# Which transfer GpSimd shares out at the start: half of dV of pair 0, or half of K of pair 2

## The chip, the cores and the metric

One NeuronCore of a Trainium2 chip. The metric is the device time of one execution in microseconds (us), taken as the median of several runs. PE is TensorE, DVE is VectorE, ACT is ScalarE, POOL is GpSimd and SP is SyncE. Sixteen DMA engines move all data between HBM and the on-chip memory (SBUF); SP's and POOL's transfers run on the same sixteen, from queues of their own. MB and KB are powers of two here where a transfer's size is meant.

## The reference

Attention of one query row per head, forward and backward, in bf16. There are 32 heads, 8192 keys each, and 128 features.

```
q: [1, 32, 1, 128]   k, v: [1, 32, 8192, 128]   grad_out: [1, 32, 1, 128]
scores = einsum('bhqd,bhkd->bhqk', q, k) * 128 ** -0.5
attn   = softmax(scores)
out    = einsum('bhqk,bhkd->bhqd', attn, v)
returns out, and the gradients dq, dk, dv of it for grad_out
```

K and V are read once (134 MB), dK and dV, of the same size, are written once. dV is the outer product of the weights with grad_out's row; dK is the outer product of the scores' gradient with q's row.

## The kernel before, in words

Heads are worked on in 16 pairs (`j`). K and V of a pair are 4 MB each and lie in SBUF as 128 partitions of 128 rows, 32 KB to a partition. Three K tiles and two V tiles rotate. dV overwrites V in place and dK overwrites K in place, in eight steps `r` of 16 rows (`outer`, L286; DVE at L290), and the result is stored from the same tile. So a tile comes free for the next load when its store has landed.

For a pair, DVE transposes K blocks (`k_blocks`, L188) and PE makes scores of them (L198). DVE, ACT and PE make the softmax (L422 to L455). PE turns V (`v_transposes`, L215; ACT copies, L220) and multiplies it with grad_out (L232). Then DVE writes dV. The scores' gradient (`ds_of`, L320) and dK follow in the next turn of the loop (`p_ = j - 1`). For the first pairs (`early`), the first half of V of pair `j` is turned between the gradient of pair `j - 1` and its dK (L401). The order is written out by hand (`tc.manual_schedule`, L126); each engine takes its instructions in that order, and the order of issue on SP is that of the program.

Transfers: K, V, dV and dK go through SP's queue, one 4 MB transfer each, or in parts where `LOADS` (L25) and `ENDS` (L18) say so: K of pair 0 in four, V of pair 0 in two, V of pair 1 in four, K of pair 2 in two; some stores in two or three. A transfer of 128 partitions gives each of the 16 DMA engines 8 partitions. The first five loads (K 0, V 0, K 1, V 1, K 2) are issued at the start (L98 to L102).

The exception is dV of pair 0. Its first half (64 of the 128 rows of each partition, 2 MB, so 16 KB from each partition) is stored by POOL, when four of the eight steps are done (L297, `share_out` at L116). Its six transfers take 39, 42, 8, 25, 10 and 4 partitions (`SHARES`, L27). The program counts on this: POOL's transfer of n partitions is spread over the largest number up to 16 that divides n, here 13, 14, 8, 5, 10 and 4 engines, beginning with the one at which a cursor stands, and moves the cursor on by as many. Between them, `turn_to` (L107) issues copies of a few bytes into `turned` that move the cursor to the engine that SHARES names first. By that count the engines 0 to 15 get

```
engine  0  1  2  3  4  5  6  7  8  9 10 11 12 13 14 15
rows   12 12 12  6  0  4  7  8  8  8  9  8  8  7  7 12      (partitions' 16 KB; 128 in all)
```

The second half of dV of pair 0 is stored by SP after the eighth step (L299). The two small outputs (out_0 and out_1, 8 KB each) are stored by POOL near the end (L404, L406, `result` at L334).

Of the kernel before, what the change touches and what calls it, by code (L numbers as in the profile page):

```python
# [18 lines left out]
CH = 16  # L19
# [2 lines left out]
K_BUFS = 3  # L22
V_BUFS = 2
QD = 32
LOADS = {("k", 0): 4, ("v", 0): 2, ("v", 1): 4, ("k", 2): 2}  # L25
SHARED = 64
SHARES = ((6, 12, 39), (5, 2, 42), (5, 1, 8), (15, 55, 25), (10, 25, 10), (7, 0, 4))  # L27
GP = 4

# [2 lines left out]
def kernel(  # L32
# [11 lines left out]
    nc = tc.nc  # L44
# [5 lines left out]
    NT = 2 * S // P  # L50
    NU = NT // CH
# [21 lines left out]
    Kt, Vt, XK, XV, st, acc, qd = {}, {}, {}, {}, {}, {}, {}  # L73

    def rows_of(x, j, c=0, parts=1):
        L = NT // parts
        return x[0, 2 * j:2 * j + 2].rearrange("b s d -> (b s) d").rearrange("(p n) d -> p n d", p=P)[:, c * L:(c + 1) * L, :]

    def slots(X, c, parts):
        L = NT // parts  # L80
        return X[:, c * L:(c + 1) * L, :]

    def load_k(j):
        parts = LOADS.get(("k", j), 1)
        Kt[j] = kpool.tile([P, NT, D], BF16, tag="K", name="Kt")
        for c in range(parts):
            nc.sync.dma_start(slots(Kt[j], c, parts), rows_of(k, j, c, parts))

    def load_v(j):
        Vt[j] = vpool.tile([P, NT, D], BF16, tag="V", name="Vt")  # L90
        parts = LOADS.get(("v", j), 1)
        for c in range(parts):
            nc.sync.dma_start(slots(Vt[j], c, parts), rows_of(v, j, c, parts))

    rows = consts.tile([H, 2, D], BF16)
    nc.scalar.dma_start(rows[:, 0, :], q.rearrange("b h s d -> (b h s) d"))
    nc.scalar.dma_start(rows[:, 1, :], grad_out.rearrange("b h s d -> (b h s) d"))
    load_k(0)  # L98
    load_v(0)
    load_k(1)  # L100
    load_v(1)
    load_k(2)  # L102

    turned = consts.tile([17, len(SHARES), 2, 2], BF16)
    cursor = [0, 0]

    def turn_to(engine):  # L107
        n = (engine - cursor[0]) % 16
        if n:
            rows = n if n > 1 else 17  # L110
            nc.gpsimd.dma_start(turned[0:rows, cursor[1]],  # L111
                                k[0, 0].rearrange("(p n) d -> p n d", p=P)[0:rows, 0:2, 0:2])
            cursor[1] += 1
        cursor[0] = engine

    def share_out(dst, src):  # L116
        for engine, first, n in SHARES:
            turn_to(engine)
            last = first + 3 * n - 2
            nc.gpsimd.dma_start(dst[first:last:3], src[first:last:3], max_dma_last_dim=8192)  # L120
            cursor[0] = (cursor[0] + max(i for i in range(1, 17) if n % i == 0)) % 16
# [14 lines left out]
    nc.gpsimd.memset(do_win[:], 0.0)  # L136
    win = consts.tile([P, NG, 2 * QD - 8], BF16)
    nc.gpsimd.memset(win[:], 0.0)
    in_quad = consts.tile([P, NQ], F32)
    nc.vector.reduce_sum(in_quad[:], ident[:].rearrange("p (a i) -> p a i", a=NQ), axis=AX.X)  # L140

# [26 lines left out]
    o_all = consts.tile([P, H], F32)  # L168
    dq_all = consts.tile([P, H], F32)
# [99 lines left out]
    def gather_copy(j, which):  # L269
        if j % GP != GP - 1:  # L270
            return
        S = acc["S" + which] = small.tile([P, 4, D], F32, tag="S", name="S_" + which)
        nc.scalar.copy(S[:].rearrange("p j d -> p (j d)"), acc.pop(which)[:])

    def gather(j, which, bank):
        if j % GP != GP - 1:
            return
        S, to = acc.pop("S" + which), (o_all if which == "p" else dq_all)
        pick = lane[:].rearrange("p (w j) -> p j w", j=4)
        at = 8 if which == "p" else 16  # L280
        for i in range(4):
            nc.tensor.matmul(bank[:, at:at + 2 * GP], lhsT=S[:, i, :], rhs=pick[:, i, :],
                             start=(i == 0), stop=(i == 3), skip_group_check=True)
        nc.scalar.copy(to[:, 2 * (j - GP + 1):2 * j + 2], bank[:, at:at + 2 * GP])

    def outer(j, which, r):  # L286
        x = st[j]
        G, dst = (Kt[j], out_2) if which == "dk" else (Vt[j], out_3)
        rep, row = x["ds"] if which == "dk" else x["p"], qd[j][:, 0 if which == "dk" else 1, :]
        nc.vector.tensor_tensor(  # L290
            slots(G, r, NU).rearrange("p n (a b) -> p n a b", b=R),
            slots(rep, r, NU).unsqueeze(2).to_broadcast([P, CH, D // R, R]),
            row.rearrange("p (a b) -> p a b", b=R).unsqueeze(1).to_broadcast([P, CH, D // R, R]),
            op=ALU.mult)
        if (which, j) == ("dv", 0):
            if (r + 1) * CH == SHARED:
                share_out(rows_of(dst, 0)[:, 0:SHARED, :], G[:, 0:SHARED, :])  # L297
            elif r == NU - 1:
                nc.sync.dma_start(rows_of(dst, 0)[:, SHARED:NT, :], G[:, SHARED:NT, :])  # L299
            return  # L300
        ends = ENDS.get((which, j), (8,))
        if r + 1 in ends:
            i = ends.index(r + 1)
            a, b = (ends[i - 1] if i else 0) * CH, (r + 1) * CH
            nc.sync.dma_start(rows_of(dst, j)[:, a:b, :], G[:, a:b, :])
# [25 lines left out]
        nc.vector.tensor_copy(x["ds"][:], ds1[:].unsqueeze(2).to_broadcast([P, NT, R]))  # L331
        window(ds1[:].rearrange("p (g j) -> p g j", j=4))

    def result(src, dst, issuer):  # L334
        half = small.tile([P, H], BF16, tag="half", name="half", bufs=2)
        nc.scalar.copy(half[:], src[:])
        fin_ps = psT.tile([P, 2 * TB, P], BF16, tag="T", name="fin_ps")
        nc.tensor.transpose(fin_ps[0:H, 0, :], half[:], ident[:])
        fin_sb = small.tile([H, D], BF16, tag="fin", name="fin_sb", bufs=2)
        nc.scalar.copy(fin_sb[:], fin_ps[0:H, 0, :])  # L340
        issuer.dma_start(dst.rearrange("b h s d -> (b h s) d"), fin_sb[:])

    DQ = NG // 4
    NC = NX // TB
# [5 lines left out]
    def half(j, f):  # L350
        for c in range(f * NC, (f + 1) * NC):
            chunk(j, c)
        v_scores(j, f)

    for j in range(HP + 1):
# [42 lines left out]
        if ends and j > 0:  # L398
            gather_copy(p_, "ds")
            if early:  # L400
                half(j, 0)  # L401
            for r in range(NU):
                if j == HP and r == NU - 2:
                    result(o_all, out_0, nc.gpsimd)  # L404
                    gather(p_, "ds", st[p_]["m"])
                    result(dq_all, out_1, nc.gpsimd)  # L406
                outer(p_, "dk", r)
            if j + 1 < HP:
                load_v(j + 1)
# [7 lines left out]
        if not ends:  # L417
            gather_copy(p_, "ds")
            outer(p_, "dk", 0)
            outer(p_, "dk", 1)  # L420
# [104 lines left out]
```

## Time and profile before

| what | value |
|---|---|
| median of 3 runs | 633.09 us (632.57 to 633.21) |
| the profiled execution: its own time | 632.87 us |
| its span, first to last instruction | 631.1 us |
| busy: PE, DVE, ACT, POOL | 73%, 82%, 32%, 2% |
| bytes moved by DMA, mean rate | 268.98 MB, 426 GB/s |
| HBM read, written | 134.23 MB, 134.23 MB |
| q1 (SP's queue): packets, MB | 11232, 266.34 |
| q0 (POOL's queue): packets, MB | 800, 2.12 |

The prediction uses the page (its slices of DMA share and GB/s, its queues), the timelines of SP, POOL and DVE, and stretches of a few us. In a timeline a line begins with its start and its length in us, then engine, source line, operation and what it writes from what; in brackets stands the engine's idle time before it and what ended that. SPq lines are issues of transfers, not the transfers themselves. A stretch shows the busy time of PE, weight loads, DVE, ACT and POOL, then TensorE's granted clock, the DMA engines' mean busy share and GB/s. Beside these the trace has a record for each DMA packet (start, length, size, queue), which doesn't name the engine but lets one follow it, since an engine's next packet starts some 3 ns before the last one's end; and 16 landing records for each transfer, one for each engine.

### The profile page before, as it was taken

The page shows a single profiled execution, that of the slowest core. Times are in us where ns is not written, and L with a number is a line of the kernel's source. Part 1 is how long each engine was busy: PE and PEld are TensorE (multiplying, and loading weights), DVE is VectorE, ACT ScalarE, POOL GpSimd, SP SyncE. Part 2 cuts the span into 40 slices and gives each one's busy share as a digit, 9 for nine tenths or more (in the row PEclk, how much of TensorE's full clock was granted, in tenths as well). Part 3 has the DMA queues.
Part 4 walks back from the last instruction along what each step waited for, and adds up shares of the span by engine and source line. Part 5 has one row for each costly group of instructions (what it writes and reads, how often), then busy time and mean ns, then how long its engine had stood idle before and what let it go on. Part 6 is the DMA issues. An engine that isn't in the chain of part 4 may idle for free.

```text
span 631.1 us, 8018 instructions
## 1 busy us (share of the span) xinstructions
PE 462.9 (73%) x3256; PEld 245.9 (39%) x3256; DVE 516.4 (82%) x654; ACT 205.1 (32%) x460; POOL 11.3 (2%) x23
## 2 busy tenths in 40 slices
PE   4887678878787788676888757867679776697671
PEld 1443344244443425233363432624336243262441
DVE  6579997989889798796879959879697895987973
ACT  2432424043342505134052330613316142160431
POOL 2040000000000000000000000000000000000000
PEclk9789987789798977788868789777897778987785
DMA  8999999999999999999999999999999999999997
GB/s 366 433 402 436 430 428 431 429 427 440 433 427 436 436 431 433 433 432 429 429 432 429 427 433 427 433 432 418 431 430 437 436 431 425 436 427 431 428 426 336
DMA packets 12164, 268.98 MB, mean 426 GB/s; under 512 B 1856, under 2 KB 1888, under 8 KB 1888
## 3 DMA queue, kind: packets, MB, share of 16 engines
q1 hardware_dynamic: 11232, 266.34, 98.5%
q0 software_dynamic: 800, 2.12, 0.8%
q8 instruction: 25, 0.41, 0.2%
q14 instruction: 11, 0.09, 0.0%
q10 hardware_dynamic: 96, 0.02, 0.0%
HBM read 134.23 MB, written 134.23 MB: 425 GB/s over the span
## 4 chain that ended last, share of the span: by engine, by line
issue 91%; DMA 3%; PE 3%; DVE 1%; ACT 0%; POOL 0%; POOLq 0%; ACTq 0%
DMA out_dram<-Vt 2%; PE s_ps L198 1%; DMA Kt<-in_k_dram 1%; PE T_ps L215 1%; PE acc_p L265 0%; DVE XK_sb L188 0%; DVE Vt L290 0%; POOL out_dram L120 0%; DVE q_blk L174 0%; ACT p_rep L452 0%; DVE sT L205 0%; ACT win L255 0%; ACT e L440 0%; POOL turned L111 0%; POOLq L520 0%
## 5 line engine op out<-in xcount | busy, mean ns | idle before, releaser
L198 PE MATMUL s_ps<-XK_sb,q_win 128*128 128x512 bf16 x512 | 152.4, 432 | 66.6 <-DVE XK_sb L188 61.3
L290 DVE TENSOR_TENSOR Vt<-p_rep,qd 128x2048 bf16<-128x2048 bf16 x128 | 154.0, 1223 | 40.1 <-PE acc_p L265 32.2
L188 DVE STREAM_TRANSPOSE XK_sb<-Kt 128x1024 f32<-128x1024 f32 x128 | 150.2, 1218 | 37.7 <-DMA Kt<-in_k_dram 35.0
L215 PE MATMUL T_ps<-ident_f,Vt 128*128 128x128 f32 x1024 | 165.4, 314 | 6.1 <-DMA Vt<-in_v_dram 6.1
L220 ACT COPY XV_sb<-T_ps 128x512 f32<-128x512 f32 x256 | 139.6, 591 | 82.6 <-PE T_ps L215 82.4
L290 DVE TENSOR_TENSOR Kt<-ds_rep,qd 128x2048 bf16<-128x2048 bf16 x128 | 149.5, 1215 | 3.2 <-PE acc_ds L265 2.8
L215 PEld LDWEIGHTS T_ps<-ident_f,Vt 128*128 128x128 f32 x1024 | 131.2, 160 | 43.8 <-issue 18.7
L198 PEld LDWEIGHTS <-q_win 128*128 128x128 bf16 x512 | 51.6, 110 | 155.6 <-issue 123.9
L265 PE MATMUL acc_p<-Vt,win 128*32 128x512 bf16 x512 | 55.9, 439 | 2.8 <-ACT win L255 2.8
L440 ACT ACTIVATE e<-sT,nbias 128x128 f32<-128x128 f32 x16 | 8.2, 515 | 150.6 <-DVE nbias L436 150.6
L265 PEld LDWEIGHTS <-win 128*32 128x32 bf16 x1024 | 23.0, 99 | 60.6 <-issue 49.4
L265 PE MATMUL acc_ds<-Kt,win 128*32 128x512 bf16 x512 | 42.7, 429 | 4.6 <-ACT win L255 4.6
L232 PE MATMUL dp_ps<-XV_sb,do_win 128*32 128x512 bf16 x512 | 34.3, 383 | 13.5 <-ACT XV_sb L220 13.5
L255 ACT COPY win<-ds 64x128 bf16<-64x128 bf16 x32 | 9.5, 296 | 106.4 <-DVE ds L327 106.2
L232 PEld LDWEIGHTS <-do_win 128*32 128x32 bf16 x512 | 14.3, 94 | 29.2 <-issue 22.5
L441 PE MATMUL m_ps<-rs,ones_f 128*128 128x1 f32 x32 | 7.5, 305 | 24.4 <-ACT e L440 24.4
L427 PE MATMUL m_ps<-ident_f,top 128*128 128x128 f32 x16 | 4.8, 300 | 23.5 <-DVE top L425 23.5
L205 DVE STREAM_TRANSPOSE sT<-s_ps 128x512 f32<-128x512 f32 x16 | 11.5, 717 | 10.7 <-PE s_ps L198 10.7
L441 PEld LDWEIGHTS m_ps<-rs,ones_f 128*128 128x128 f32 x32 | 6.2, 242 | 27.6 <-ACT e L440 27.6
L452 ACT ACTIVATE p_rep<-e,rinv 128x512 bf16<-128x512 f32 x16 | 11.5, 722 | 13.3 <-DVE rinv L450 13.3
L427 PEld LDWEIGHTS m_ps<-ident_f,top 128*128 128x128 f32 x16 | 2.1, 133 | 31.0 <-issue 25.4
L317 PEld LDWEIGHTS m_ps<-pd,ones_f 128*128 128x128 f32 x32 | 8.2, 276 | 10.6 <-DVE prod L248 9.8
(60 smaller groups left out, 158.1 us busy)
## 6 DMA issues: line engine op xcount, KB each, us to landing
Kt<-in_k_dram SPq DMA_DIRECT2D x14, 4096.0 KB, 29.1
Vt<-in_v_dram SPq DMA_DIRECT2D x14, 4096.0 KB, 29.0
out_dram<-Kt SPq DMA_DIRECT2D x13, 4096.0 KB, 25.1
out_dram<-Vt SPq DMA_DIRECT2D x13, 4096.0 KB, 32.3
out_dram<-Vt SPq DMA_DIRECT2D x5, 2048.0 KB, 16.2
out_dram<-Kt SPq DMA_DIRECT2D x5, 2048.0 KB, 15.7
Kt<-in_k_dram SPq DMA_DIRECT2D x4, 1024.0 KB, 8.2
Vt<-in_v_dram SPq DMA_DIRECT2D x2, 2048.0 KB, 17.5
```

The source lines that it names most:

```text
L188: nc.vector.transpose(XK[j, u][:].rearrange("p g w i -> p (g w i)"), slots(Kt[j], u, NU).rearrange("p g d -> p (g d)").bitcast(F32))
L198: nc.tensor.matmul(st[j]["s"][:], lhsT=q_win[:, c, at:at + P], rhs=cols[:, c // 2, c % 2], start=(u == 0 and c == 0), stop=(u == NU - 1 an ...
L205: nc.vector.transpose(sT[:].rearrange("p g r -> p (g r)"), x["s"][:])
L215: nc.tensor.transpose(T_ps[:, i, :], words[:, m * P:(m + 1) * P], ident_f[:])
L220: nc.scalar.copy(XV[j][:, b * TB:(b + 1) * TB, :], st[j].pop(("T", c))[:])
L232: nc.tensor.matmul(out[b * QD:(b + 1) * QD, :], lhsT=do_win[:, b // 2, e2, at:at + QD], rhs=cols[:, z, e2, :, b * QD:(b + 1) * QD], start= ...
L255: nc.scalar.copy(win[t * M:(t + 1) * M, :, at:at + 4], src[t * M:(t + 1) * M])
L265: nc.tensor.matmul(acc[which][b * QD:(b + 1) * QD, :], lhsT=win[:, g, at:at + QD], rhs=X[:, 4 * g:4 * g + 4, :].rearrange("p n d -> p (n d)"),
L290: nc.vector.tensor_tensor(slots(G, r, NU).rearrange("p n (a b) -> p n a b", b=R), slots(rep, r, NU).unsqueeze(2).to_broadcast([P, CH, D // ...
L317: nc.tensor.matmul(x["m"][:, 1:3], lhsT=ones_f[:], rhs=x["pd"][:], start=True, stop=True, skip_group_check=True)
L441: nc.tensor.matmul(x["m"][:, 0:1], lhsT=ones_f[:], rhs=rs[:], start=True, stop=True, skip_group_check=True)
L452: nc.scalar.activation(x["p"][:], e[:].unsqueeze(2).to_broadcast([P, NT, R]), ACT.Copy, scale=rinv[:])
```

## The change

POOL no longer stores anything. It loads the second half of K of pair 2 (64 rows of each partition, 2 MB) with the same `SHARES`, the same cursor copies and the same partitions, right after its memsets at the start, where it waits for nothing else. SP loads only the first half of that tile, in one transfer. dV of pair 0 is stored whole by SP after the eighth step, like other dV. V of pair 1 is loaded in one transfer, no longer four, and V of pair 0 in four, no longer two. The two small outputs are stored by SP: out_0 and out_1 stand between the second and the third part of the last dK store in SP's order.

SP's order at the start becomes K 0 in four parts, V 0 in four, K 1, V 1, half of K 2, dV 0, dK 0, V 2, and then as before. The instructions of PE, DVE and ACT are the same in number and order.

```diff
-LOADS = {("k", 0): 4, ("v", 0): 2, ("v", 1): 4, ("k", 2): 2}
+LOADS = {("k", 0): 4, ("v", 0): 4}
 SHARED = 64
+SHARED_K = 2
...
     def load_k(j):
         parts = LOADS.get(("k", j), 1)
         Kt[j] = kpool.tile([P, NT, D], BF16, tag="K", name="Kt")
+        if j == SHARED_K:
+            nc.sync.dma_start(Kt[j][:, 0:NT - SHARED, :], rows_of(k, j)[:, 0:NT - SHARED, :])
+            return
...
-    def share_out(dst, src):
+    def share(dst, src):
...
     nc.gpsimd.memset(win[:], 0.0)
+    share(Kt[SHARED_K][:, NT - SHARED:NT, :], rows_of(k, SHARED_K)[:, NT - SHARED:NT, :])
...
-        if (which, j) == ("dv", 0):
-            if (r + 1) * CH == SHARED:
-                share_out(rows_of(dst, 0)[:, 0:SHARED, :], G[:, 0:SHARED, :])
-            elif r == NU - 1:
-                nc.sync.dma_start(rows_of(dst, 0)[:, SHARED:NT, :], G[:, SHARED:NT, :])
-            return
...
-    def result(src, dst, issuer):
+    def result(src, dst):
...
-        issuer.dma_start(dst.rearrange("b h s d -> (b h s) d"), fin_sb[:])
+        nc.sync.dma_start(dst.rearrange("b h s d -> (b h s) d"), fin_sb[:])
...
-                    result(o_all, out_0, nc.gpsimd)
+                    result(o_all, out_0)
...
-                    result(dq_all, out_1, nc.gpsimd)
+                    result(dq_all, out_1)
```

## The prediction, made before the change was run

> **What bounds it now.** I read the page's slices first, then the DMA part, the windows of the two places where the rate falls, and the timelines of SP (SyncE, the queue that issues), POOL and DVE.
>
> ```profile
> span 631.1 us, 8018 instructions
> ...
> DMA  8999999999999999999999999999999999999997
> GB/s 366 433 402 436 430 428 431 429 427 440 433 427 436 436 431 433 433 432 429 429 432 429 427 433 427 433 432 418 431 430 437 436 431 425 436 427 431 428 426 336
> ...
> q1 hardware_dynamic: 11232, 266.34, 98.5%
> q0 software_dynamic: 800, 2.12, 0.8%
> ```
>
> The 16 DMA engines are busy in every slice, at 425 to 440 GB/s in nearly all; DVE, the next, is at 82%. Only three slices are lower: first, third, last. So the time is the bytes (268.98 MB in both kernels), plus what an engine stands idle, plus how unevenly the 16 finish. The chain of waits tells nothing here (91% "issue"). q0 is GpSimd's queue, q1 SyncE's.
>
> ```profile
> 34.00:36.00 2.00, 2.00 (x20) 1.25 (x18) 1.87 (x2) 1.69 (x4) 2.00 (x4) 1.00 1.03 348
> 36.00:38.00 2.00, 1.60 (x20) 1.09 (x20) 1.74 (x3) 1.53 (x3) 0.92 (x2) 1.00 0.98 356
> ...
> 626.00:628.00 2.00, 0.00 (x0) 0.00 (x0) 0.00 (x0) 0.00 (x0) 0.00 (x0) 0.50 0.65 279
> 628.00:630.00 2.00, 0.00 (x0) 0.00 (x0) 0.00 (x0) 0.00 (x0) 0.00 (x0) 0.50 0.19 82
> ```
>
> The last two columns are the DMA engines' busy share and GB/s. At 34 to 38 us, where GpSimd's transfers begin, the engines are busy yet slow: (4 - 2*348/430 - 2*356/430) = 0.7 us lost by all. At the end they finish one by one. The trace's landing records (16 for a transfer, one an engine) of the last store run from 626.7 to 630.2, middle 628.2.
>
> **What the share does.** SyncE's transfers give each engine the same bytes; GpSimd's do not. By SHARES, engines 0, 1, 2 and 15 get 12 rows of 16 KB, most of the others 7 to 9, engine 3 gets 6, engine 5 gets 4 and engine 4 none. The landing records agree: those of one transfer spread over 0.7 us up to 22 us, and over 7.1 us from 57 us on, with one engine about 3 us ahead of the next. I call it the front engine. In the packet records it takes 1246 ns for 32 KB of a store where the others take 1213, so it falls back 8*33 = 0.27 us in each 4 MB store, 8.6 us over 32 stores. Its last landing is 629.4, the twelfth of 16. So the share is a head start that the front engine has used up at the end; moving it from 32 us to 4 us changes neither its rows nor the sum.
>
> **Part by part.**
>
> 1. *Bytes and packet sizes.* Per engine and 4 MB, start to start in the packet records: 32 packets of 8 KB by 0.306 = 9.79 us; 16 of 16 KB by 0.610 = 9.76; 8 of 32 KB by 1.210 = 9.68. V of pair 0 goes from 16 to 8 KB: +0.03. V of pair 1 from 8 to 32 KB: -0.11. K of pair 2 has half of its 16 KB turned to GpSimd's 8 KB: +0.02; dV of pair 0 goes from half 8, half 16 to 32 KB: -0.10. Sum **-0.16 us**.
>
> 2. *The share itself.* The same 12 issues of GpSimd, with the same rows, in the same order, so 0.7 us of slow packets again, now at about 7 to 9 us. The trace has no shared load, only shared stores; bounds are -0.7 (a load doesn't do it) and +0.7 (twice as much). I take **0**: the slow packets were SyncE's own, ahead of the first shared byte at 36.3.
>
> 3. *What the share delays at the start.* GpSimd now has nothing to wait for but its memsets:
>
> ```profile
> 3.44 0.73 POOL L111 DMA_DIRECT2D turned<-in_k_dram  x1
> 32.13 0.65 POOL L120 DMA_DIRECT2D out_dram<-Vt  x1 [27.97 <-DVE Vt L290]
> ...
> 36.35 0.57 POOL L111 DMA_DIRECT2D turned<-in_k_dram  x1
> 41.53 0.56 POOL L120 DMA_DIRECT2D out_dram<-Vt  x1 [4.61 <-DMA out_dram<-Vt]
> ```
>
> Its first share is issued at 3.44+0.73 = 4.2 and, with the 4.2 us from issue (32.13) to first byte (36.3), moves from 8.3 on. In the packet records from 36 us on an engine alternates: one packet of q0, one of q1, 1:1, where q0's small packets (cursor copies, completions) take a turn but only 9 ns. Engine 0 gets six 8 KB packets, 3 small ones, six, about 5 small, ten, and so on. K of pair 0 lands in four parts, at 5.8, 8.4, 10.8 and 13.3 us. At 8.3 the slowest engine has some 6.5 packets of part 3 to go and 8 of part 4. Part 3: 6 of q0 in between, 10.8 + 6*0.306 + 0.7 (point 2) = 13.4. Part 4: 12 of q0 ahead of its last, 13.3 + 12*0.306 + 0.7 = 17.7.
>
> ```profile
> 12.70 2.37 DVE L188 STREAM_TRANSPOSE XK_sb<-Kt 128x1024 f32<-128x1024 f32 x2 [0.15 <-PE s_ps L198]
> 15.82 2.37 DVE L188 STREAM_TRANSPOSE XK_sb<-Kt 128x1024 f32<-128x1024 f32 x2 [0.74 <-PE s_ps L198]
> 19.31 0.72 DVE L205 STREAM_TRANSPOSE sT<-s_ps 128x512 f32<-128x512 f32 x1 [1.12 <-PE s_ps L198]
> ```
>
> Part 3 is used at 12.70 and part 4 at 15.82, so all computing shifts by D = 17.7 - 15.82 = **1.9 us**. Ends: 0.5 (the share comes late) and 5.5 (all 24 packets, 7.3 us, ahead of part 4: 13.3+7.3+0.7-15.82). I take 1.9, as the alternation is in the records. [...]
>
> 4. *Who hides D: the backlog in the rings.* SyncE's issues are early; the question is whether one comes after the front engine has run dry (its landing, the first of 16, less the 0.5 us that the record lags) less 1.0 us from issue to first packet (0.74 to 1.75 at the start).
>
> ```profile
> 38.77 0.35 SPq L299 DMA_DIRECT2D out_dram<-Vt  x1
> 52.89 0.34 SPq L305 DMA_DIRECT2D out_dram<-Kt  x1
> 65.04 0.34 SPq L93 DMA_DIRECT2D Vt<-in_v_dram  x1
> 73.17 4.87 SPq L305 DMA_DIRECT2D out_dram<-Vt  x2
> ```
>
> The front engine has no share, so it is dry at the same bytes in both kernels: after 18 MB at 47.5, 22 MB at 57.8, 30 MB at 77.5 (landings). dV of pair 0, whole: may come at 46.0, comes at 38.8+D. dK of pair 0: 56.3 against 52.9+D. dV of pair 1: 76.0 against 73.2+D. So the cover is 7.2, 3.4 and **2.8 us**, later 5.0 (dK 1), 3.1 (dV 2) and 3.7 (dK 2), and from 147 us on over 8. The other engines have 2.4 us more (4 rows). V of pair 2 (65.0 against 66.3) waits for the landing of dV 0 on the slowest engine; that engine has had the same bytes, so it stays. Were the cover gone, the front engine's end moves by D-2.8, and 0.8 of that is free (629.4 against 630.2). At D = 1.9: **0**.
>
> 5. *V of pair 1 whole.* PE turns its first half at 46.5+D = 48.4; whole, it lands on engine 0 at 1.9 + 64*0.306 + 24*0.306 + 2*9.68 + 0.7 + 0.5 = 49.4. PE waits 1 us, behind it the scores of pair 1; those wait for DVE, busy with dK of pair 0 to 52.8+D, and PE was done 1.7 us before DVE. Hidden: **0**.
>
> 6. *The two small outputs* go from POOL's queue to SP's, ahead of the last dK store. SP then issues that at 620.3+0.4 to +0.8. The first five engines run dry at about 621.4 and idle up to 0.8 us; they landed 3 us before the last: **0**.
>
> **Sum.** -0.16 on the profiled execution: its span is 631.1 and its time 632.87 (1.8 around it), so **632.7 us**. The median of the three runs is 633.09; a difference under 0.2% (1.3 us) is about what can't be told from none.
>
> **Rivals.**
>
> *Starved front engine (slower).* The share gets ahead of part 4. Against: 1:1 alternation. For: the issue comes while q1 has 8 KB packets, and contention at 34 to 38 us is not understood. It decides from D = 2.8+0.8 = 3.6; at D = 5.5 the end is 1.9 us later: 634.6.
>
> *The load sprays otherwise (slower).* The head starts hang on the engine at which a shared transfer begins, and on how many it uses. Before shows this for stores only. If a load with n rows begins at engine 0 with n/16 rows each, rounded up, the front engine gets 3+3+1+2+1 = 10 rows, 10*0.61 = 6.1 us: it ends at 635.5 in place of 630.2, in all 632.87+5.3 = 638.2. Against: the small "turned" copies are loads, and moved the cursor as counted. [...]
>
> *A better share (faster).* The slow packets of 34 to 38 us go (-0.7) and the last engines land nearer the middle (630.2 against 628.2, so at most -1.9): with -0.16 and half of the second, 631.0. For: nothing is stored while the share moves. Against: the rows are the same.
>
> *Worse balance at the end (slower).* The instruction fetches, 16 KB packets that cost their engine 0.9 us each, meet other engines than before; two more on the last engine: 634.5.
>
> **Numbers.** Forecast 0.52, all of it within 0.2%; starved 0.15; other spray 0.10; better share 0.15; worse balance 0.08. Faster 0.15, same 0.52, slower 0.33. The range runs from 631.0 to 636.0: it leaves out the other spray and some of the better share.
>
> **What would show it.** DVE's first transposes of part 4 at about 17.7; landings of the first V of pair 0 spread by several us; the front engine some 7 us ahead by 30 us; dK of pair 0 issued near 54.8 and no slice under 420 GB/s after the second; last landings again over some 3.5 us, ending near 630. An idle front engine between 57 and 78 us, or another order of finishing, would make it wrong.

## The result, and the profile after

The changed kernel takes **643.84 us** (median; 643.33 to 645.03) where the kernel before took 633.14 on the same chip. The ratio is 1.0172, 95% interval 1.0159 to 1.0185: slower by 10.7 us. I had forecast 632.7 us, no change, with a range from 631.0 to 636.0.

The page of the kernel after: its span, the DMA part of the slices, the two large queues.

```profile
span 642.0 us, 8013 instructions
...
DMA  8999999999999999999999999999999999999996
GB/s 296 269 391 433 432 419 435 435 432 429 430 432 434 433 428 434 432 431 430 438 433 428 429 429 432 430 429 436 434 429 426 429 434 436 427 430 432 425 427 293
...
q1 hardware_dynamic: 11040, 266.36, 97.9%
q0 software_dynamic: 736, 2.10, 1.2%
```

The bytes are the same 268.98 MB, and the DMA engines are as busy as before. But in the first three slices they move 296, 269 and 391 GB/s, where before had 366, 433 and 402; from the fourth on all is as it was. q0 takes 1.2% of the engines' span, where nearly the same bytes cost 0.8% before: its packets last longer. Stretches of four us show where this begins and ends (columns as before: the last two are the DMA engines' busy share and GB/s).

```profile
4.00:8.00 4.00, 0.80 (x4) 0.40 (x4) 2.32 (x3) 0.90 (x4) 4.00 (x8) 1.00 1.02 426
8.00:12.00 4.00, 2.77 (x7) 1.00 (x8) 2.81 (x11) 0.26 (x1) 0.90 (x2) 1.00 1.04 295
...
16.00:20.00 4.00, 2.06 (x8) 0.77 (x8) 1.30 (x2) 0.00 (x0) 0.47 (x1) 1.00 1.03 264
...
32.00:36.00 4.00, 2.41 (x15) 1.67 (x14) 2.09 (x2) 1.73 (x5) 0.00 (x0) 0.65 1.02 264
36.00:40.00 4.00, 3.87 (x26) 2.12 (x28) 2.11 (x2) 1.76 (x3) 0.00 (x0) 0.50 1.08 440
```

```profile
8.00:36.00 28.00, 16.96 (x74) 7.79 (x75) 12.45 (x24) 6.69 (x19) 2.62 (x5) 0.89 1.03 275
```

And the same 28 us of the kernel before:

```profile
8.00:36.00 28.00, 23.25 (x141) 12.45 (x141) 17.57 (x28) 11.27 (x28) 3.87 (x7) 0.88 1.01 424
```

The slow stretch begins with the first shared packet (8.1 us in the packet records) and ends with the last (35.5). The second block takes it as one: 275 GB/s, where the kernel before has 424. The loss is 28*(1 - 275/430) = **10.1 us**. It falls on both queues: between 8 and 36 us a packet of 8 KB took 471 ns on average in GpSimd's queue and 488 ns in SyncE's, where before had averages of 311 and 313 at 38 to 60 us.

What the engines compute is late as well. First SP's issues after, then DVE's transposes of the third and fourth part of K of pair 0:

```profile
47.38 0.35 SPq L304 DMA_DIRECT2D out_dram<-Vt  x1
65.34 0.34 SPq L304 DMA_DIRECT2D out_dram<-Kt  x1
...
86.12 4.88 SPq L304 DMA_DIRECT2D out_dram<-Vt  x2
```

```profile
14.93 2.37 DVE L193 STREAM_TRANSPOSE XK_sb<-Kt 128x1024 f32<-128x1024 f32 x2 [2.54 <-DMA Kt<-in_k_dram]
21.39 2.37 DVE L193 STREAM_TRANSPOSE XK_sb<-Kt 128x1024 f32<-128x1024 f32 x2 [4.09 <-DMA Kt<-in_k_dram]
```

Part 4 is used at 21.4 us (before 15.8, forecast 17.7), and dV of pair 0 goes out at 47.4 (before 38.8, forecast 40.7). Most of this comes free, because the DMA engines are late by as much and the rings (the engines' queues) do not run dry: from 40 to 615 us the packet records show fewer than 16 packets under way for only 0.3 us in all. The front engine alone falls back. Its lead over the middle landing shrinks by 1.0 us at 98 us and by 0.4 at 108, and its last packets there are longer: 1007 and 1208 ns for 16 KB, where 611 is usual, and 1533 for 32 KB, where 1213 is. Why these packets are long is not shown. At the end the 16 landings of the last store run from 636.6 to 641.1, middle 637.9. The middle is 9.7 us later than before (628.2), the last landing 10.9 (630.2). So about 10 us are the slow packets, and about 1 us the wider spread at the end.

### The profile page after: what moved, and what is told of

Its sections match the earlier page's. It is cut to its first block, busy times and chain, and to the rows that moved or that the text cites. A ratio compares the mean times of both kernels' runs of the same rounds, so it can differ in the third digit from the quotient of the medians.

```text
span 642.0 us, 8013 instructions
## 1 busy us (share of the span) xinstructions
PE 466.0 (73%) x3256; PEld 248.7 (39%) x3256; DVE 516.2 (80%) x654; ACT 204.9 (32%) x460; POOL 10.0 (2%) x21
## 2 busy tenths in 40 slices
DMA packets 11908, 268.98 MB, mean 419 GB/s; under 512 B 1888, under 2 KB 1888, under 8 KB 1888
## 4 chain that ended last, share of the span: by engine, by line
DMA 57%; PE 23%; DVE 14%; ACT 3%; issue 1%; DVEq 0%; ACTq 0%; SPq 0%
DMA Vt<-in_v_dram 32%; DMA out_dram<-Vt 15%; PE T_ps L220 12%; DMA Kt<-in_k_dram 7%; DVE Kt L295 5%; PE s_ps L203 5%; DVE Vt L295 4%; PE acc_p L270 3%; DVE XK_sb L193 3%; DMA out_dram<-Kt 3%; ACT XV_sb L225 2%; PE dp_ps L237 2%; PE acc_ds L270 1%; DMA rows<-in_grad_out_dram 1%; DVE sT L210 1%
## 5 line engine op out<-in xcount | busy, mean ns | idle before, releaser
L203 PE MATMUL s_ps<-XK_sb,q_win 128*128 128x512 bf16 x512 | 155.0, 440 | 72.0 <-DVE XK_sb L193 67.4
L220 PE MATMUL T_ps<-ident_f,Vt 128*128 128x128 f32 x1024 | 168.4, 318 | 8.1 <-DMA Vt<-in_v_dram 8.1
L220 PEld LDWEIGHTS T_ps<-ident_f,Vt 128*128 128x128 f32 x1024 | 134.8, 163 | 45.7 <-issue 21.4
L270 PE MATMUL acc_p<-Vt,win 128*32 128x512 bf16 x512 | 56.2, 442 | 2.9 <-ACT win L260 2.9
L237 PEld LDWEIGHTS <-do_win 128*32 128x32 bf16 x512 | 14.5, 95 | 29.3 <-issue 22.9
```

What stands on the lines that cost most here:

```text
L203: nc.tensor.matmul(st[j]["s"][:], lhsT=q_win[:, c, at:at + P], rhs=cols[:, c // 2, c % 2], start=(u == 0 and c == 0), stop=(u == NU - 1 an ...
L220: nc.tensor.transpose(T_ps[:, i, :], words[:, m * P:(m + 1) * P], ident_f[:])
L237: nc.tensor.matmul(out[b * QD:(b + 1) * QD, :], lhsT=do_win[:, b // 2, e2, at:at + QD], rhs=cols[:, z, e2, :, b * QD:(b + 1) * QD], start= ...
L270: nc.tensor.matmul(acc[which][b * QD:(b + 1) * QD, :], lhsT=win[:, g, at:at + QD], rhs=X[:, 4 * g:4 * g + 4, :].rearrange("p n d -> p (n d)"),
```

## The experiments

Three theories stood at the start, and two came later; the expectations name them by letters. **A**: a transfer is slow while it writes SBUF partitions into which another DMA engine is loading at the same time. **B**: any GpSimd load beside SyncE's loads slows both. **C**: the cursor copies or the uneven shares do it. **P**, a sharper A: the partitions fall into sets of eight, each of which takes about what one DMA engine brings; time is lost when two engines write into one set at once, whatever their queue. **F**: an engine that writes partitions other than those it gets in a transfer of 128 (call those its own, the others foreign) is slow by itself. Each kernel starts from the one after, and each ratio is to the kernel before, measured on the same chip. In the one after, a shared transfer takes every third partition of a range (`dst[first:last:3]` in `share`), so by the program's count the partitions that fall to an engine are not those of a transfer of 128.

**1. No share.** K of pair 2 is loaded whole by SyncE.

```diff
-        if j == SHARED_K:
-            nc.sync.dma_start(Kt[j][:, 0:NT - SHARED, :], rows_of(k, j)[:, 0:NT - SHARED, :])
-            return
...
-    share(Kt[SHARED_K][:, NT - SHARED:NT, :], rows_of(k, SHARED_K)[:, NT - SHARED:NT, :])
```

> The changed kernel without the share: K of pair 2 whole by SP, POOL moves nothing; every engine gets the same bytes. Three theories for the 10.7 us that the change cost, all in the stretch from 8 to 36 us where the DMA rate fell from 430 to about 270 GB/s. A, foreign partitions: a shared load writes partitions that another engine's load is writing at the same time. B, two load queues: any load of POOL beside SP's loads slows both. C, the cursor copies and uneven transfers of POOL. All three expect 430 GB/s from 8 to 36 us here, and the front engine (slow on stores) to end 8 rows * 0.61 = 4.9 us later than before the change: about 637 us. So a shared load would be worse than no share.

Measured: 636.79 us, ratio 1.0058 (1.0043 to 1.0073).

```profile
8.00:12.00 4.00, 2.87 (x7) 1.00 (x8) 2.81 (x10) 0.26 (x1) 0.00 (x0) 1.00 1.01 426
```

The last landings run from 629.5 over 4.6 us, with one engine last by 1.9 us, as is to be expected of the front engine without its head start. So the share as a load costs 7 us against no share at all, and the share as a store, with the parts that the loads had before, had brought 3.7.

**2. The share as a store again,** with the other edits of the change kept.

```diff
+        if (which, j) == ("dv", 0):
+            if (r + 1) * CH == SHARED:
+                share(rows_of(dst, 0)[:, 0:SHARED, :], G[:, 0:SHARED, :])
+            elif r == NU - 1:
+                nc.sync.dma_start(rows_of(dst, 0)[:, SHARED:NT, :], G[:, SHARED:NT, :])
+            return
```

(and experiment 1's edit)

> The changed kernel with the share put back to the first half of dV of pair 0, as before; the rest of the change stays (V of pair 0 in four parts, V of pair 1 in one, K of pair 2 in one, small outputs by SP). A, B and C: all the loss goes, 632.7 us within 1.3, and 430 GB/s from 8 to 30 us. If the parts of loads or the outputs' queue cost anything, it shows here: 634 or more.

Measured: 644.48 us, ratio 1.018 (1.0165 to 1.0196). A miss, and not for the reason of the changed kernel: from 8 to 30 us the rate is 439 GB/s, as before. SP's issue of V of pair 2, and the stretches beside it:

```profile
76.11 0.34 SPq L94 DMA_DIRECT2D Vt<-in_v_dram  x1
```

```profile
66.00:70.00 4.00, 3.33 (x40) 1.92 (x40) 3.20 (x4) 3.32 (x9) 0.00 (x0) 1.00 0.91 379
70.00:74.00 4.00, 3.61 (x37) 1.82 (x34) 4.00 (x4) 2.04 (x6) 0.00 (x0) 1.00 0.56 174
74.00:78.00 4.00, 2.10 (x10) 0.87 (x8) 3.45 (x8) 0.00 (x0) 0.00 (x0) 1.00 0.48 129
```

Here the busy share falls too (0.56, 0.48): the engines are idle. V of pair 2 is issued at 76.1, before at 65.0, as it waits for dV of pair 0 to leave its tile. In the packet records of before the two queues alternate packet by packet: of GpSimd's 256 packets of 8 KB, 186 have a single packet that starts 2 to 5 ns before their end, and in all 186 cases it is SyncE's, 104 of 8 KB, 57 of 16 KB and 25 of 4 bytes. V of pair 1 and K of pair 2 now have packets of 32 KB; if 1:1 holds there too, GpSimd's 8 KB get a fifth of an engine's bytes in place of a half or a third (an estimate from the sizes). The share lasts until 75.3 us. The three stretches lose 5.7 us against 430 GB/s. Since all engines stand idle for the same transfer there, the head start is gone as well: the first landings after it, at 89 us, lie within 0.7 us. By experiment 1 a head start is worth 3.7 us. The remaining 2 of the 11 us I did not follow.

**3. The same with V of pair 1 in four parts and K of pair 2 in two,** as in the kernel before, so packets of 8 and 16 KB.

```diff
-LOADS = {("k", 0): 4, ("v", 0): 4}
+LOADS = {("k", 0): 4, ("v", 0): 4, ("v", 1): 4, ("k", 2): 2}
```

> The kernel with the shared store and whole loads lost 11 us in a second way: its loads of V 1 and K 2 had 32 KB packets, POOL's queue got one 8 KB packet or one small one to each of these, the share ended at 76 us in place of 63, and V of pair 2 was issued at 76.1 in place of 65.0. Here those two loads go back to four and two parts (8 and 16 KB packets), as before the change; V of pair 0 in four parts and the outputs by SP stay. If the packets' size is the cause: V of pair 2 at 65 and 632.9 us within 1. If the outputs or V of pair 0 take part: over 634.

Measured: 633.09 us, ratio 1.0002 (0.9993 to 1.0011); V of pair 2 is issued at 65.15. So the packets' size was the cause in experiment 2: here the share's last 8 KB packet ended at 58.7 us, there at 75.3. V of pair 0 in four parts and the small outputs by SP, which this kernel keeps, cost nothing.

**4. GpSimd loads the same half in one transfer of 128 partitions.**

```diff
-    share(Kt[SHARED_K][:, NT - SHARED:NT, :], rows_of(k, SHARED_K)[:, NT - SHARED:NT, :])
+    nc.gpsimd.dma_start(Kt[SHARED_K][:, NT - SHARED:NT, :], rows_of(k, SHARED_K)[:, NT - SHARED:NT, :], max_dma_last_dim=8192)
```

> POOL loads the same half of K of pair 2, at the same place, in one transfer of 128 partitions: each engine writes its own 8 partitions, 8 KB packets, no cursor copies, no head start. A: 430 GB/s from 8 to 20 us and the time of the kernel without a share, about 637. B: about 270 GB/s for as long as both queues load, 4 MB in 15.5 in place of 9.8 us, so about 643. C: as A.

Measured: 637.48 us, ratio 1.0066 (1.0051 to 1.0081), within 0.7 us of no share. The stretches:

```profile
8.00:12.00 4.00, 2.44 (x6) 0.85 (x7) 2.91 (x11) 0.26 (x1) 0.00 (x0) 1.00 1.01 428
12.00:16.00 4.00, 3.33 (x15) 1.29 (x14) 1.89 (x2) 1.30 (x6) 0.00 (x0) 1.00 1.01 426
```

GpSimd's 256 packets move from 7.5 to 17.7 us beside SyncE's at full rate, 310 ns each. B falls.

**5. The same in two transfers of 64 partitions,** the lower half, then the upper.

```diff
+    for h in (slice(0, 64), slice(64, 128)):
+        nc.gpsimd.dma_start(Kt[SHARED_K][h, NT - SHARED:NT, :], rows_of(k, SHARED_K)[h, NT - SHARED:NT, :], max_dma_last_dim=8192)
```

> POOL loads the same half of K of pair 2 in two transfers of 64 partitions each, 4 partitions to an engine: same bytes to each engine as in one transfer of 128, no cursor copies, but each engine now writes partitions that another engine's load writes at the same time. A: about 270 GB/s from 8 to 22 us and about 643 us. B: the same as the one transfer of 128, whatever that gives. C: 430 GB/s and about 637.

Measured: 646.42 us, ratio 1.0219 (1.0199 to 1.024).

```profile
8.00:12.00 4.00, 2.67 (x7) 0.98 (x8) 2.91 (x11) 0.26 (x1) 0.00 (x0) 1.00 1.02 236
12.00:16.00 4.00, 3.33 (x12) 0.97 (x11) 0.50 (x1) 0.76 (x3) 0.00 (x0) 1.00 1.02 238
```

Equal shares, no cursor copies, and 236 GB/s: C falls as the cause. What differs from experiment 4 is the partitions that a transfer spans, and that there are two transfers; experiment 7 parts these.

**6. Other rows of HBM.** As experiment 4, but from rows of K 64 partitions further on; the second half of K of pair 2 is other data here.

```diff
+    far = k[0].rearrange("b s d -> (b s) d").rearrange("(p n) d -> p n d", n=NT)
+    at = SHARED_K * P + P // 2
+    nc.gpsimd.dma_start(Kt[SHARED_K][:, NT - SHARED:NT, :], far[at:at + P, NT - SHARED:NT, :], max_dma_last_dim=8192)
```

> As the one POOL transfer of 128 partitions, but each partition is filled from the HBM rows that belong 64 partitions further on, so that each engine writes its own partitions and reads other engines' HBM rows; the second half of K of pair 2 is then not K of pair 2, so what is computed of pair 2 changes, and its time not. If the slow stretch comes from partitions of SBUF that another engine's load is writing (A): 430 GB/s from 8 to 18 us, about 637 us. If it comes from the HBM side, from rows that another engine reads: about 245 GB/s and about 646, as with two transfers of 64.

Measured: 636.73 us, ratio 1.0063 (1.0043 to 1.0083).

```profile
8.00:12.00 4.00, 2.70 (x7) 1.00 (x8) 2.81 (x11) 0.26 (x1) 0.00 (x0) 1.00 1.01 430
```

So here it did not count which engine read which rows of HBM (430 GB/s, and 428 in experiment 4). A transfer of 64 consecutive partitions also reads a narrower stretch of HBM (2 MB, where every second partition spans 4); experiments 10 and 11 bear on that.

**7. Even and odd partitions.** As experiment 5, but the 64 partitions of a transfer are every second one.

```diff
+    for h in (slice(0, 128, 2), slice(1, 128, 2)):
+        nc.gpsimd.dma_start(Kt[SHARED_K][h, NT - SHARED:NT, :], rows_of(k, SHARED_K)[h, NT - SHARED:NT, :], max_dma_last_dim=8192)
```

> GpSimd loads the second half of K of pair 2 as two transfers of 64 partitions, as in the kernel with two halves (646.4 us), but the first takes the even partitions and the second the odd ones. A transfer of 64 partitions gives each engine four of them in order, so here every engine writes only the partitions that are its own in a transfer of 128. Transfers, packets and queues are those of the two halves. A (foreign partitions cost the time): 430 GB/s from 8 us on and 637 us. Rival (transfers of 64 partitions cost it, by their number, their order or their descriptors): some 250 GB/s from 8 to 24 us and 646 us.

Measured: 636.98 us, ratio 1.0063 (1.0046 to 1.008).

```profile
8.00:12.00 4.00, 2.42 (x6) 0.85 (x7) 2.81 (x11) 0.26 (x1) 0.00 (x0) 1.00 1.01 428
```

Two transfers of 64 partitions, full rate: 428 GB/s in place of 236, for nothing but the choice of partitions (and of the rows that go with them). (Which engine writes which partition is not in the trace. That the partitions fall to the engines in order is my expectation's own count; by P, experiment 10 speaks against it.)

**8. The shared load later,** beside stores: issued at 42 us, with dV and dK of pair 0 stored in four parts each, so that packets are of 8 KB.

```diff
-ENDS = {("dv", 1): (4, 8), ...
+ENDS = {("dv", 0): (2, 4, 6, 8), ("dk", 0): (2, 4, 6, 8), ("dv", 1): (4, 8), ...
...
+        if j == 0:
+            flag = consts.tile([P, 1], BF16)
+            nc.gpsimd.tensor_copy(flag[:], ds1[:, 0:1])
+            share(Kt[SHARED_K][:, NT - SHARED:NT, :], rows_of(k, SHARED_K)[:, NT - SHARED:NT, :])
```

> The shared load as changed, with all its unequal shares and foreign partitions, but issued at about 43 us (POOL first copies one column of the gradient of pair 0), so that it moves from 47 us on, beside SP's stores of dV 0 and dK 0 (8 KB packets, four parts each) in place of loads. A, a load conflicts only with a load: full rate of 430 GB/s from 47 to 70 us, the head start is kept, 633 us within 2. If a shared load slows whatever lies beside it: a stretch near 270 GB/s and about 643.

Measured: 636.32 us, ratio 1.0057 (1.0039 to 1.0076).

```profile
46.00:50.00 4.00, 3.84 (x32) 3.32 (x32) 4.00 (x5) 3.41 (x8) 1.14 (x2) 1.00 0.93 350
50.00:54.00 4.00, 1.84 (x20) 0.81 (x20) 4.00 (x4) 0.60 (x2) 0.99 (x2) 1.00 1.02 414
54.00:58.00 4.00, 3.62 (x16) 1.28 (x15) 4.00 (x5) 0.00 (x0) 0.72 (x2) 1.00 1.01 416
```

While SyncE's last loads are still running (until 49.7 us) the rate is 350 GB/s. Once SyncE only stores, the shared load runs beside it at 414 to 416, and from 50 to 62 us each of its packets took 309 ns. So writing foreign partitions was not slow by itself (against F): the same packets took 471 ns on average beside loads in the changed kernel. The time missed the expectation's upper end by 1.3 us: the front engine falls behind its pace (landings of a part at 50.0, 52.8, 56.2 and 59.0 us, where 2.45 us apart is full speed, 8 packets of 0.306 us), the landings of dK of pair 0 are spread over 5.4 us at 67 us, where before has 7.0, and the last landing is at 633.9. Why it runs short there I did not settle.

**9. SyncE loads the half itself in two halves;** GpSimd loads nothing.

```diff
+            for h in (slice(0, 64), slice(64, 128)):
+                nc.sync.dma_start(Kt[j][h, NT - SHARED:NT, :], rows_of(k, j)[h, NT - SHARED:NT, :])
```

> GpSimd loads nothing; SyncE loads the second half of K of pair 2 itself, as two transfers of 64 partitions (the lower, then the upper ones) right behind the first half. Each engine again writes foreign partitions, but all from one queue. If it takes two queues to lose time, the rate stays at 430 GB/s and the time is that without a share, 637 us. If the partitions of one engine take only about what one engine brings, whatever the queue, then 16 engines writing into the partitions of 8 move some 215 GB/s: 2 MB take 9.8 us in place of 4.9, the rate falls to about half in one stretch of 10 us near 35 to 50 us, and the time is about 641 to 642 us.

Measured: 642.37 us, ratio 1.0151 (1.0136 to 1.0166).

```profile
42.00:46.00 4.00, 4.00 (x36) 1.83 (x29) 3.78 (x4) 0.00 (x0) 0.00 (x0) 0.50 1.02 432
46.00:50.00 4.00, 4.00 (x29) 3.67 (x28) 4.00 (x4) 3.36 (x7) 0.00 (x0) 0.81 1.10 250
50.00:54.00 4.00, 2.44 (x23) 1.07 (x23) 4.00 (x5) 0.85 (x2) 0.00 (x0) 1.00 1.03 221
```

No second queue was needed: 221 GB/s with SyncE alone. From 47 to 55 us the 16 KB packets took a median of 1265 ns where 611 is usual: half the rate, as P would have it for 16 engines on the partitions of eight.

**10. The same in four quarters of 32 partitions.**

```diff
+            for h in (slice(0, 32), slice(32, 64), slice(64, 96), slice(96, 128)):
```

> As the kernel in which SyncE loads the second half of K of pair 2 in two halves of 64 partitions (642.4 us), but in four quarters of 32 consecutive partitions. If the sets that take what one engine brings are consecutive eights, 16 engines write into four of them: some 105 GB/s, the 2 MB take 19.6 us in place of 4.9, and the time is about 651 us. If 32 consecutive partitions reach as many sets as 64 do, the rate is 205 GB/s for 9 us as with the halves and the time 642 us. [...]

Measured: 642.1 us, ratio 1.014 (1.0125 to 1.0155).

```profile
50.00:54.00 4.00, 2.93 (x24) 1.21 (x24) 4.00 (x4) 0.23 (x1) 0.00 (x0) 1.00 1.00 213
```

A quarter of the partitions runs as fast as a half (213 and 221 GB/s), so, read by P, 32 consecutive partitions reach as many sets as 64, and the sets are not consecutive eights. Which partitions make up a set no run shows.

**11. One transfer of the partitions 8 to 127, then one of 0 to 7,** by SyncE.

```diff
+            for h in (slice(8, 128), slice(0, 8)):
```

> GpSimd loads nothing. SyncE loads the second half of K of pair 2 as one transfer of the partitions 8 to 127 and one of the partitions 0 to 7. 120 partitions make 15 engines with eight in order, so each writes only foreign partitions, those of its neighbour, and no two write the same engine's at once. Theory P (a set of eight partitions takes about what one engine brings; time is lost when two engines write into one set in the same moment, whoever they are): 425 GB/s or more but at the seams, and 637 to 638 us. Rival F (an engine that writes foreign partitions is slow by itself): the rate falls as in the kernel with two halves by SyncE (205 GB/s for 9 us), and 641 to 642 us. The same would come if the sets of partitions are not consecutive eights.

Measured: 643.74 us, ratio 1.0163 (1.0146 to 1.018).

```profile
46.00:50.00 4.00, 3.19 (x31) 2.66 (x32) 4.00 (x4) 3.90 (x8) 0.00 (x0) 1.00 1.06 238
50.00:54.00 4.00, 2.11 (x21) 0.86 (x21) 4.00 (x5) 0.00 (x0) 0.00 (x0) 1.00 1.02 238
```

P's number was wrong: it was worked out for sets of consecutive eights, which experiment 10 rules out. So this run does not tell P from F; experiment 8 does. It does speak against a narrow stretch of HBM as the cause: 120 partitions read nearly all of the 4 MB and are slow (238 GB/s), and the quarters of experiment 10, which read 1 MB each, are hardly slower than the halves (213 and 221).

**12. One foreign writer.** No share, but GpSimd first loads a little of the tile, which SyncE then loads whole: 17 partitions of 8 KB, by the program's count all on one engine.

```diff
+    nc.gpsimd.dma_start(Kt[2][0:17, 0:32, :], rows_of(k, 2)[0:17, 0:32, :], max_dma_last_dim=8192)
+    nc.sync.dma_start(Kt[2][:], rows_of(k, 2))
```

> No share; one small POOL transfer of 17 partitions, 8 KB each, that a single engine moves from about 8 us on (SP's whole load of K of pair 2 follows it and writes the same again). The question is how far one foreign writer reaches. If it slows only the one engine whose partitions it writes: from 8 us the rate falls by at most 2 of 16, to 400 GB/s or more. If it holds up all: under 330 GB/s until its 17 packets are through, some 10 to 17 us. The time is near 637 in the first case, 1 to 4 us more in the second.

Measured: 639.63 us, a single run. Inconclusive: the 17 packets did not go through one engine (six were under way at once at 7.4 us), so the question of a single foreign writer was not answered. These few packets still took the rate to 303 GB/s from 8 to 10 us, a loss of 0.6 us for all engines.

## Why the prediction was wrong

- **Step 2, the share itself, failed.** I took 0 and gave bounds of 0.7 us either way, "The same 12 issues of GpSimd, with the same rows, in the same order". It was 10.1 us. The issues were the same, but the direction was not: the share of before reads SBUF while SyncE's loads write it; the changed one writes SBUF beside loads that write it. I had noted that the trace had no shared load, and then bounded it by the row of shared stores, which could not hold the cost. Experiments 4, 5 and 7 show that the loss hangs on which partitions a transfer takes (428, 236 and 428 GB/s from 8 to 12 us), 8 that the shared load ran at 414 to 416 GB/s once nothing else loaded, and 9 that the loss needs no second queue (221).
- **Why one foreign writer at a time is enough** is argued from P, not shown. An estimate from the rates: 430 GB/s are 27 for each of 16 engines, and the 221 and 213 of experiments 9 and 10 are what eight engines bring at that rate. If a set takes hardly more than one engine brings, there are 16 sets, and a half or a quarter of the partitions reached eight. Then an engine that alternates between its own set and another's would meet a second writer now and then, while some other set stands idle. A second estimate: if each of 16 engines wrote into one of 16 sets at random, 1 - (15/16)^16 = 64% of the sets would be busy at any time; measured were 275/430 = 64%. The agreement may be luck, since every other packet of an engine goes to its own set and not to one at random. SyncE's own packets became as slow as GpSimd's (488 and 471 ns); by what way no run shows.
- **Step 3, D.** The alternation 1:1 was right: in experiment 4 the same bytes at full rate bring part 4 in at a median of 18.0 us, and 13.3 + 14.5*0.306 = 17.7 was to be expected (14.5 turns of SyncE's remain at 8 us). That all computing shifts by D was too simple: in experiment 4 it is 3.0 us at DVE (18.75 against 15.78 without a share) but 0.8 at the issue of dV of pair 0 (39.6 against 38.8). In the changed kernel it was 5.6 us at DVE (21.4 against 15.8) and grew to 8.6 at dV of pair 0, as V of pair 0 came through the slow stretch too.
- **Step 4, the cover,** held in experiment 4, whose time is close to that of no share (637.5 and 636.8), and in the changed kernel as well, since the slow packets held the rings back too. The front engine lost about 1.4 us of its lead there, in long packets and without a gap between them, so that the rival "starved front engine" happened is not shown; what this loss is worth at the end was not measured apart.
- **Steps 1 and 6** were right as far as seen: experiment 3 keeps V of pair 0 in four parts and the outputs by SP, and is at 1.0002. A sum of -0.16 us is too small to be seen.
- **Step 5, V of pair 1 whole,** was not tested apart with the load; experiment 1 has it whole and comes out at the 637 us that were expected of it. With the share as a store, it and K of pair 2 whole cost 11 us together (experiments 2 and 3), by a way that the step did not have: beside packets of 32 KB the share's 8 KB packets ran until 75.3 us, in experiment 3 until 58.7.
- **The other spray** did not happen: the landings spread by 7.5 us at 50 us, as the divisor count gives. **A better share** did not happen either. **Worse balance** was in part right by its number, 4.5 us at the end in place of 3.5; whether by the instruction fetches was not followed.
- Of what would show it, the landings and the head start came as written; DVE's 17.7, the 54.8 of dK of pair 0, "no slice under 420 GB/s" and the end near 630 did not. The third is the one that pointed at step 2.

## What to carry to other kernels

To give DMA engines unequal work, let them store unequally while the rest loads: in this kernel the uneven store came out at 633.09 us (experiment 3), while the uneven load took over a third of the bandwidth from all sixteen for as long as it lasted (275 GB/s from 8 to 36 us, before 424). That it let two engines write into the same set of partitions at once is P's reading, not shown. Where a load must be split, split it so that each transfer still spans all 128 partitions, or every second one, as in experiments 4 and 7 (428 GB/s each), and not a consecutive half or quarter (221 to 236 and 213 in experiments 5, 9 and 10). And when a transfer is moved, bound its cost by a row of the same direction beside the same traffic; where there is none, the bounds must reach as far as the bandwidth that it could take.

## What the runs showed that I had not expected

- Two queues shared an engine by packets, not by bytes: beside 32 KB packets the last 8 KB packet of a 2 MB share ended at 75.3 us, beside 8 and 16 KB at 58.7, and that moved the time from 633.1 to 644.5 us.
- Consecutive 32 and 64 partitions loaded at much the same 213 and 221 GB/s, 64 even ones beside SyncE's loads at 428, as one transfer of 128 did.
- The first byte of a GpSimd transfer came 3.9 us after its issue in the changed kernel (issue 4.13, first packet 8.08) and 4.3 in experiment 8, while the rings were full. No run shows it with an idle ring.
- The slow stretch of the changed kernel did not show in the DMA engines' busy share: it stayed at 1.02 to 1.04 while the rate fell to 264 GB/s. Only GB/s and the packets' lengths (471 and 488 ns for 8 KB, before 311 and 313) told.
